# Strassen's algorithm for the second product of a fused attention and feed-forward kernel

## The chip, the cores and the metric

The kernel runs on one core of a Trainium2 chip. TensorE multiplies into PSUM (the memory of its results), VectorE and ScalarE work on the results, and in the traces the matmuls of TensorE, and the instructions of VectorE, ran in the order in which the program issued them: in the kernel before, the matmuls of M piece 0 end at 396.70, ScalarE copies its half, and VectorE comes to the other half at 399.74, behind the chain issued before it. The metric is the device time of one execution in microseconds. A profiled execution gives the trace; its span, from first to last instruction, is about 1.8 us shorter than the time. The profiler also records the clock granted to TensorE, as a share of full speed; in the traces it is 1.00 or 0.50 at any time.

In the views PE is TensorE, PEld its loads of weights, DVE VectorE, ACT ScalarE and POOL GpSimd; L408 is line 408 of that run's kernel. A line of a timeline gives start, length, engine, line, operation, tile written <- tiles read, shapes and count, then in brackets the idle time before it and what ended that.

## The reference, cut to what matters

```python
# x: (8, 8, 512, 64), state: (8, 8, 32, 64)     B, H, S, D and 32 states
xread = softmax(x @ state.T / 8) @ state         # every token reads the states
sread = softmax(state @ x.T / 8) @ x             # every state reads the tokens
t = concat([xread, sread])                       # per batch 512 + 32 tokens of 8 * 64 = 512
h = t @ w_in                                     # (4352, 512) @ (512, 2048)
out = (h * sigmoid(1.702 * h)) @ w_out           # second product: (4352, 2048) @ (2048, 512)
```

Everything is float32.

## The kernel before

The first product of a batch doesn't multiply the tokens by `w_in`. It multiplies the states by `w_in` first (the tiles M, four pieces a batch) and then the softmax weights by M. The second product is a plain sum over 16 pieces G of the hidden layer, one PSUM buffer of 128x512 for each of four row blocks of 128 tokens:

```python
def down(key, r, fs, dst, last):
    ...
    for f in fs:
        nc.tensor.matmul(ops, G[key, f][:, P * r : P * (r + 1)], w_out[:, f],
                         start=(f == 0), stop=(f == NF - 1))       # 128x128 by 128x512
    if fs[-1] == NF - 1:
        nc.scalar.copy(osb, ops)
        nc.gpsimd.dma_start(dst, osb)
```

The attention of the next batch is threaded into this product. It is cut into 16 slots, each behind four pieces of one row block:

```python
at(0, att_state, b)                  # transpose of the states
for j in range(NPR): at(1 + j, att_xT, b, j)
at(5, att_scores, b); at(5, att_blocks, b); at(5, att_s_max, b); at(5, att_s_exp, b)
at(5, att_x_exp, b); at(5, att_s_norm, b); at(5, att_x_norm, b)    # softmax, mostly on VectorE
for c in range(NFC - 1): at(7 + c, att_M, b, c)                    # M pieces 0, 1, 2
for g in range(NG): at(11 + g, att_eT, b, g)
at(14, att_sread, b)
```

Each piece of M fills two PSUM buffers, which the attention work shares (there are only two; the scores alone have others), and is copied out by VectorE and ScalarE in turn:

```python
def copies(b, i):
    return nc.scalar.copy if b in (0, 1) or i % 2 else nc.vector.tensor_copy

def att_M(b, c):
    ...
    ps = [att_ps([P, FC], f"M_{b}_{c}_{g}") for g in range(NG)]    # 2 buffers in all
    by_state(b, ps, lambda rows, j: w_in[c][rows, j])              # 16 matmul instructions of 64x32
    for g in range(NG):
        copies(b, g)(m[:, g], ps[g])                               # g = 0: VectorE, g = 1: ScalarE
```

Of the kernel before, what the change touches and what calls it, by code (L numbers as in the profile page):

```python
# [10 lines left out]
FP32 = mybir.dt.float32  # L11
I32 = mybir.dt.int32
U32 = mybir.dt.uint32
AF = mybir.ActivationFunctionType
ALU = mybir.AluOpType
# [5 lines left out]
def kernel(  # L21
# [23 lines left out]



    nc = tc.nc

    B, H, S, D = x.shape  # L50
    Ns = state.shape[2]
    DM = H * D
    DF = moe_w_in.shape[1]
    P = 128
    NPR = P // Ns
    NG = H // NPR
    NF = DF // P
    SCH = S // P
    ST = S + Ns
    FC = 512  # L60
    NFC = DF // FC
    NB = S // Ns
    scale = float(1.0 / np.sqrt(D))
    eps = 1e-9
    assert (NG * D, NPR * Ns, NPR * P, DM, NFC) == (P, P, DM, FC, SCH)

    out_x = out.rearrange("(b t) n -> b t n", b=B)[:, :S].rearrange("b (c q) n -> b c q n", c=SCH)
    out_s = out.rearrange("(b t) n -> b t n", b=B)[:, S:]
# [1 line left out]
    st_v = state.rearrange("b (j g) n d -> b g j n d", g=NG)  # L70

    konst = ctx.enter_context(tc.tile_pool(name="konst", bufs=1))
    xpool = ctx.enter_context(tc.tile_pool(name="xpool", bufs=2))
    apool = ctx.enter_context(tc.tile_pool(name="apool", bufs=1))
    mpool = ctx.enter_context(tc.tile_pool(name="mpool", bufs=3))
    wpool = ctx.enter_context(tc.tile_pool(name="wpool", bufs=2))
    gpool = ctx.enter_context(tc.tile_pool(name="gpool", bufs=1))
    opool = ctx.enter_context(tc.tile_pool(name="opool", bufs=2))
    psA = ctx.enter_context(tc.tile_pool(name="psA", bufs=2, space=bass.MemoryType.PSUM))
    psH = ctx.enter_context(tc.tile_pool(name="psH", bufs=2, space=bass.MemoryType.PSUM))  # L80
    psO = ctx.enter_context(tc.tile_pool(name="psO", bufs=4, space=bass.MemoryType.PSUM))
# [8 lines left out]



    free = [gpool.tile([P, S], FP32, name=f"g_{i}") for i in range(NF + 9)]
    zeros = free[-1].bitcast(mybir.dt.bfloat16)[:, :FC]
    nc.vector.memset(zeros, 0.0)
    one = konst.tile([P, 1], FP32, name="one")
# [9 lines left out]
    xn, stn = {}, {}  # L106
# [4 lines left out]
            nc.sync.dma_start(stn[b][:, g], st_v[b, g])  # L111

    def load_x(b):
        xn[b] = xpool.tile([P, SCH, H, D], FP32, tag="xn", name=f"xn_{b}")
        for c in range(SCH):
            queue = nc.scalar if b == 0 and c % 2 else nc.sync
            queue.dma_start(xn[b][:, c], x_v[b, c])
# [6 lines left out]
    w_out = konst.tile([P, NF, DM], FP32, name="w_out")  # L124
    w_in_words, w_out_words = moe_w_in.bitcast(I32), moe_w_out.bitcast(I32)

    PIECES = [("i", c, k) for c in range(NFC) for k in range(NPR)] + [("o", f) for f in range(NF)]
    raw, power = {}, {}
    AHEAD = 3

    def load_weight(i):

        key = PIECES[i]
        nin, room = NFC * NPR, NF // 2
        if i < room or nin - NPR <= i < nin:
            o = 2 * (i % room if i < room else i - (nin - NPR))
            raw[i] = w_out[:, o : o + 2].rearrange("p f n -> p (f n)").bitcast(I32)
        else:
            raw[i] = wpool.tile([P, 2 * FC], I32, tag="raw", name="raw_" + "_".join(map(str, key)), bufs=4)
        if key[0] == "i":  # L140
            _, c, k = key
            src = w_in_words[P * k : P * (k + 1), 2 * FC * c : 2 * FC * (c + 1)]
        else:
            src = w_out_words[P * key[1] : P * (key[1] + 1)]
        nc.sync.dma_start(raw[i], src)
# [7 lines left out]
    for i, v in enumerate((8.0 * most, 8.0 * (most - least))):  # L153
        t = konst.tile([P, 1], FP32, name=f"edge_{i}")
# [3 lines left out]
    def words(i):  # L158
        w = raw[i].rearrange("p (n w) -> p w n", w=2)
        return w[:, 0].bitcast(U32), w[:, 1]  # L160

    def round_a(i):

        _, hi = words(i)
        sc = wpool.tile([P, FC], I32, tag="sc", name=f"sc_{i}", bufs=AHEAD + 1)
        power[i] = sc
        nc.vector.tensor_scalar(sc, hi, 0x7FF00000, None, ALU.bitwise_and)
        if PIECES[i][0] == "o":
            nc.vector.tensor_scalar(sc, sc, most, least, ALU.min, ALU.max)
            nc.vector.tensor_scalar(sc, sc, -least, 8.0, ALU.add, ALU.mult)  # L170
            return
        nc.scalar.activation(out=sc.bitcast(FP32), in_=sc, func=AF.Relu, bias=edge[0], scale=-8.0)
        nc.scalar.activation(out=sc, in_=sc.bitcast(FP32), func=AF.Relu, bias=edge[1], scale=-1.0)  # L173

    def round_b(i):
        key = PIECES[i]
        dst = w_in[key[1]][:, key[2]] if key[0] == "i" else w_out[:, key[1]]
        fr = dst.bitcast(I32)
        lo, hi = words(i)
        sc = power.pop(i)  # L180

        nc.vector.tensor_scalar(fr, hi, 0xFFFFF, 0x100000, ALU.bitwise_and, ALU.bitwise_or)
        nc.vector.scalar_tensor_tensor(sc, hi, -0x80000000, sc, ALU.bitwise_and, ALU.bitwise_or)  # L183
        nc.vector.scalar_tensor_tensor(dst, lo, 2.0**-32, fr, ALU.mult, ALU.add)  # L184
        nc.vector.scalar_tensor_tensor(dst, dst, 2.0**-20, sc.bitcast(FP32), ALU.mult, ALU.mult)  # L185
        del raw[i]

    done = {"load": 0, "a": 0, "b": 0, "credit": 0.0}

    def load_weights(upto):  # L190
        while done["load"] < min(upto, len(PIECES)):
            load_weight(done["load"])
            done["load"] += 1

    def powers_to(n):
        while done["a"] < min(n, len(PIECES)):
            load_weights(done["a"] + 1)
            round_a(done["a"])
            done["a"] += 1

    def round_to(n, ahead=AHEAD):

        while done["b"] < min(n, len(PIECES)):
            powers_to(min(done["b"] + 1 + ahead, max(NFC * NPR, done["b"] + 1)))
            round_b(done["b"])
            done["b"] += 1
            if done["b"] > NPR:
                load_weights(done["b"] + 2 * NPR)

    def pace(pieces):  # L210

# [13 lines left out]
    A = {b: {} for b in range(B)}  # L225
# [33 lines left out]
    def att_blocks(b):  # L259

        a = A[b]
        t = apool.tile([P, NG, NB, Ns], FP32, tag="e1", name=f"e1_{b}")
        a["e1"] = t
# [27 lines left out]

    NS1 = NG * NB

# [57 lines left out]

    def att_slots(b):

        slots = [[] for _ in range(4 * SCH)]

        def at(i, fn, *args):
            slots[i].append((fn, args))

        at(0, att_state, b)
        for j in range(NPR):  # L360
            at(1 + j, att_xT, b, j)
        at(5, att_scores, b)
        at(5, att_blocks, b)
        at(5, att_s_max, b)
        at(5, att_s_exp, b)
        at(5, att_x_exp, b)
        at(5, att_s_norm, b)
        at(5, att_x_norm, b)
        for c in range(NFC - 1):
            at(7 + c, att_M, b, c)  # L370
        for g in range(NG):
            at(11 + g, att_eT, b, g)
        at(14, att_sread, b)
        return slots


    G = {}
# [10 lines left out]
    def up_x(b, f, spare=False):  # L388
        c, o = divmod(P * f, FC)
        m = A[b]["M", c]  # L390
        up(b, f, S, [m[:, g, o : o + P] for g in range(NG)], [A[b]["aT"][:, g] for g in range(NG)], spare)

    def up_s(f):
        up(
            "sr", f, B * Ns,
            [w_in_of(k, f) for k in range(NPR)],
            [srT[:, k].rearrange("p b n -> p (b n)") for k in range(NPR)],
        )
# [3 lines left out]
    def down(key, r, fs, dst, last):  # L402

        if fs[0] == 0:
            O[key, r] = psO.tile([P, DM], FP32, tag="o", name=f"o_{key}_{r}")
        ops = O[key, r]
        for f in fs:
            nc.tensor.matmul(  # L408
                ops, G[key, f][:, P * r : P * (r + 1)], w_out[:, f], start=(f == 0), stop=(f == NF - 1)
            )  # L410
            if last:
                free.append(G.pop((key, f)))
        if fs[-1] == NF - 1:
            osb = opool.tile([P, DM], FP32, tag="osb", name=f"osb_{key}_{r}")
            nc.scalar.copy(osb, ops)  # L415
            nc.gpsimd.dma_start(dst, osb)  # L416


    nper = FC // P
# [75 lines left out]
    for f in range(NF):  # L495
# [11 lines left out]
        if f % 2 == 1:  # L507
            up_x(1, rest.pop(0))
    load_state(2)
    load_x(2)  # L510

    nb = P // Ns
    for b in range(1, B):
        ahead = b + 1 < B
        slots = att_slots(b + 1) if ahead else [[]] * (4 * SCH)
        if not ahead:
            for f in range(NF):
                up_s(f)
            for r in range(B // nb):
                for i in range(4):  # L520
                    down("sr", r, range(4 * i, 4 * i + 4), out_s[nb * r : nb * (r + 1)], r == B // nb - 1)
        if b > 1:
            for f in range(NF):
                if f == 2 * nper:
                    att_M(b, NFC - 1)
                up_x(b, f)
        for u in range(4 * SCH):
            r, i = divmod(u, 4)
            down(b, r, range(4 * i, 4 * i + 4), out_x[b, r], r == SCH - 1)
            for fn, args in slots[u]:  # L530
                fn(*args)
        if b + 2 < B:
            load_state(b + 2)
            load_x(b + 2)
# [30 lines left out]
```

## Time and profile before

| | before |
|---|---|
| time, median (lowest to highest) | 862.65 us (862.49 to 864.99) |
| TensorE busy | 98% of the span |
| second product, 7 batches | 54.9 us each |
| second product, states | 27.5 us |
| one batch, from second product to second product | 95.0 us |
| granted TensorE clock, mean | 0.996 |

TensorE's busy time says little of its speed: the ends of matmuls are modelled, and neighbours overlap in the listing (the states' second product, listed from 743.88 for 27.63 us, would end at 771.51, and the next product starts at 771.34). So durations of a stage are read here as differences of starts. The 95.0 us are 269.98 - 174.99, two starts of a batch's second product. The lines themselves are in the prediction.

### The profile page before, as it was taken

The numbers are of one execution on the slowest core, as the hardware profiler recorded it, in microseconds if no ns is written. First come the engines' busy times: TensorE is split into PE (matmuls) and PEld (weight loads), VectorE is DVE, ScalarE is ACT, GpSimd is POOL, SyncE is SP. The second block draws the span as 40 slices with busy tenths as digits, with TensorE's granted clock in tenths as the row PEclk, the third lists the DMA queues.
The fourth block names the chain that finished last, engine by engine and source line by source line (L and its number), as shares of the span: only waits on it lengthen the run. The fifth ranks groups of instructions, "written<-read, shape, count | busy, mean of one in ns | idle before, by whom it ended". The sixth has DMA issues, their size and how long they took to land.

```text
span 860.6 us, 6881 instructions
## 1 busy us (share of the span) xinstructions
PE 841.0 (98%) x2898; PEld 391.0 (45%) x2900; DVE 215.9 (25%) x402; ACT 205.5 (24%) x347; POOL 19.8 (2%) x42
## 2 busy tenths in 40 slices
PE   8987999999999999999999999999999999999997
PEld 3332554443544445443544445443544348644443
DVE  4996996005000320005000510014000500000000
ACT  3686211012032212302041212302131202103100
POOL 0000000010000000000000000000000000000000
PEclk9999999999999999999999999999999999999999
DMA  9620345010030002000020002000000000000000
GB/s 246 248 82 17 123 150 125 1 64 13 12 62 4 12 25 61 1 16 13 25 49 4 24 13 62 0 13 12 17 8 4 22 12 13 1 14 11 12 12 25
DMA packets 43135, 35.05 MB, mean 41 GB/s; under 512 B 36832, under 2 KB 36832, under 8 KB 43104
## 3 DMA queue, kind: packets, MB, share of 16 engines
q1 hardware_dynamic: 37920, 25.17, 10.7%
q0 software_dynamic: 3104, 8.92, 2.9%
q10 hardware_dynamic: 2080, 0.52, 0.3%
q8 instruction: 23, 0.38, 0.2%
q14 instruction: 8, 0.07, 0.0%
HBM read 25.69 MB, written 8.91 MB: 40 GB/s over the span
## 4 chain that ended last, share of the span: by engine, by line
issue 72%; PE 21%; DVE 2%; POOL 2%; ACT 2%; DMA 1%; SPq 0%; POOLq 0%; ACTq 0%
PE o L408 11%; PE h L383 7%; POOL out_dram L416 2%; PE M L252 1%; PE sr L341 1%; DMA xn<-in_x_dram 1%; PE xT L244 0%; ACT M L324 0%; PE s L252 0%; ACT e L282 0%; DVE w_in L185 0%; DVE w_in L184 0%; DVE sc L183 0%; PE warm L103 0%; ACT sc L173 0%
## 5 line engine op out<-in xcount | busy, mean ns | idle before, releaser
L408 PE MATMUL o<-w_out,g 128*128 128x512 f32 x1024 | 456.9, 595 | 0.0
L408 PEld LDWEIGHTS o<-w_out,g 128*128 128x128 f32 x1024 | 188.6, 190 | 231.7 <-issue 230.3
L383 PE MATMUL h<-aT,M 128*128 128x512 f32 x512 | 227.2, 599 | 9.3 <-ACT M L324 9.3
L383 PEld LDWEIGHTS h<-aT,M 128*128 128x128 f32 x512 | 96.6, 191 | 136.8 <-issue 113.2
L385 ACT ACTIVATE g<-h 128x512 f32<-128x512 f32 x128 | 76.3, 597 | 157.0 <-PE h L383 156.9
L324 DVE COPY M<-M 128x512 f32<-128x512 f32 x24 | 16.4, 682 | 194.6 <-PE M L252 194.6
L415 ACT COPY osb<-o 128x512 f32<-128x512 f32 x32 | 18.8, 586 | 136.3 <-PE o L408 134.0
L324 ACT COPY M<-M 128x512 f32<-128x512 f32 x40 | 22.6, 587 | 66.7 <-PE M L252 66.7
L252 PE MATMUL M<-w_in,stT 64*32 64x512 f32 x512 | 37.8, 601 | 0.4 <-DVE w_in L185 0.4
L416 POOL DMA_DIRECT2D out_dram<-osb x32 | 17.6, 549 | 782.4 <-ACT osb L415 782.2
L245 ACT COPY xT<-xT 128x512 f32<-128x512 f32 x18 | 10.5, 586 | 92.3 <-PE xT L244 92.3
L235 DVE COPY stT<-stT 128x128 f32<-128x128 f32 x6 | 1.8, 292 | 119.5 <-PE stT L233 119.5
L341 PEld LDWEIGHTS sr<-eT,xn 128*128 128x128 f32 x256 | 29.8, 192 | 3.8 <-issue 3.8
L341 PE MATMUL sr<-eT,xn 128*128 128x64 f32 x256 | 29.4, 273 | 0.0
L245 DVE COPY xT<-xT 128x512 f32<-128x512 f32 x14 | 9.7, 692 | 74.5 <-PE xT L244 74.5
L383 PE MATMUL h_sr<-srT,w_in 128*128 128x256 f32 x128 | 27.8, 379 | 0.0
L408 PE MATMUL o_sr<-w_out,g 128*128 128x512 f32 x64 | 27.6, 592 | 0.0
L383 PEld LDWEIGHTS h_sr<-srT,w_in 128*128 128x128 f32 x128 | 24.3, 190 | 3.7 <-issue 0.5
L244 PEld LDWEIGHTS xT<-ident,xn 128*128 128x128 f32 x128 | 16.0, 143 | 17.2 <-issue 13.5
L265 DVE STREAM_TRANSPOSE e<-s 128x512 f32<-128x512 f32 x16 | 10.5, 695 | 47.4 <-PE s L252 47.4
L103 PE MATMUL warm<-g 128*128 128x512 bf16 x74 | 20.9, 431 | 1.5 <-DVE one L97 1.2
L350 DVE COPY srT<-sr 64x128 f32<-64x128 f32 x6 | 1.7, 283 | 81.4 <-PE sr L341 81.4
(63 smaller groups left out, 355.2 us busy)
## 6 DMA issues: line engine op xcount, KB each, us to landing
raw_o<-in_moe_w_out_dram SPq DMA_DIRECT2D x16, 512.0 KB
out_dram<-osb POOLq DMA_DIRECT2D x32, 256.0 KB, 2.3
xn<-in_x_dram SPq DMA_DIRECT2D x30, 256.0 KB
w_out<-in_moe_w_in_dram SPq DMA_DIRECT2D x12, 512.0 KB
raw_i<-in_moe_w_in_dram SPq DMA_DIRECT2D x4, 512.0 KB
stn<-in_state_dram SPq DMA_DIRECT2D x16, 32.0 KB
xn<-in_x_dram ACTq DMA_DIRECT2D x2, 256.0 KB
out_dram<-osb_sr POOLq DMA_DIRECT2D x2, 256.0 KB, 7.1
```

The costliest lines, as they stand in the source:

```text
L103: nc.tensor.matmul(ps, zeros[:, :P], zeros, start=True, stop=True)
L244: nc.tensor.transpose(ps[:, c], x_heads(b, c, j), ident)
L245: copies(b or None, j)(A[b]["xT"][:, j], ps.rearrange("p c q -> p (c q)"))
L252: nc.tensor.matmul(ps[g][st], A[b]["stT"][rows, st], rhs(rows, j), start=True, stop=True)
L265: nc.vector.transpose(t[:, g].rearrange("p i n -> p (i n)"), a["s"][g])
L324: copies(b, g)(m[:, g], ps[g])
L341: nc.tensor.matmul(ps[:, j], x_heads(b, c, j), a["eT"][:, :, c, Ns * j : Ns * (j + 1)], start=(c == 0), stop=(c == SCH - 1),)
L383: nc.tensor.matmul(hps, lhs[i], rhs[i], start=(i == 0), stop=(i == n - 1))
L385: nc.scalar.activation(out=gt[:, :ntok], in_=hps, func=AF.Gelu_apprx_sigmoid)
L408: nc.tensor.matmul(ops, G[key, f][:, P * r : P * (r + 1)], w_out[:, f], start=(f == 0), stop=(f == NF - 1))
L415: nc.scalar.copy(osb, ops)
L416: nc.gpsimd.dma_start(dst, osb)
```

## The change

Strassen's algorithm (in its form with 15 sums) splits tokens, hidden layer and output columns in half and does seven products of halves where the plain form does eight. The sums of quarters of G are made by VectorE for each batch, those of `w_out` once, in float32. Batch 0 keeps the plain form, because its pieces of `w_out` are still being converted while it runs. The core of the diff:

```diff
+    def sums_of_g(key, f, ntok):
+        half = ntok // 2
+        (a11, a21), (_, a22) = quarters(key, f, ntok), quarters(key, HF + f, ntok)
+        s1, s2 = S1[:, f, :half], S2[:, f, :half]
+        nc.vector.tensor_tensor(out=s1, in0=a21, in1=a22, op=ALU.add)
+        nc.vector.tensor_tensor(out=a21, in0=a11, in1=a21, op=ALU.subtract)
+        nc.vector.tensor_tensor(out=s2, in0=s1, in1=a11, op=ALU.subtract)
+
+    def strassen(key, ntok, dst, slots=None):
...
+        def product(ps, lhs, rhs, first):
+            for r in range(nb):                       # 2 row blocks
+                for f in range(HF):                   # 8 pieces, 128x128 by 128x256
+                    nc.tensor.matmul(ps[:, r], lhs[f][:, P * r : P * (r + 1)], rhs[:, f],
+                        start=(first and r == 0 and f == 0), stop=(f == HF - 1), skip_group_check=True)
+                if todo:
+                    for fn, args in todo.pop(0):
+                        fn(*args)                     # attention slots of the next batch
...
+        X = bank("x"); product(X, A(0, 0), B11, True);  nc.scalar.copy(k1, X)
+        Y = bank("y"); product(Y, S(S2), T2, True);     k2 = Y + k1
+        product(X, A(0, 1), B21, False);                store(0, 0, X, None)
+        for f in range(HF): a12[f] -= S2[f]
+        product(Y, A(1, 0), T3, False);                 k3 = Y + k1
+        Z = bank("z"); product(Z, S(S1), T1, True);     store(1, 1, Z, k3)
+        product(Y, A(1, 1), T4, False);                 store(1, 0, Y, k1)
+        product(Z, A(0, 1), B22, False);                store(0, 1, Z, k2)
...
-        slots = [[] for _ in range(4 * SCH)]
+        slots = [[] for _ in range(14)]
...
-            at(1 + j, att_xT, b, j)
+            at(j, att_xT, b, j)
...
-        for c in range(NFC - 1):
-            at(7 + c, att_M, b, c)
+        at(5, att_M, b, 0)
+        at(7, att_M, b, 1)
+        at(9, att_M, b, 2)
         for g in range(NG):
-            at(11 + g, att_eT, b, g)
-        at(14, att_sread, b)
+            at(10 + g, att_eT, b, g)
+        at(12, att_sread, b)
...
+    for t, x0, x1 in ((T1, B12, B11), (T2, B22, T1), (T4, B21, T2), (B12, B22, B12)):
+        nc.vector.tensor_tensor(out=t, in0=x0, in1=x1, op=ALU.subtract)
+    for f in range(HF):
+        sums_of_g(1, f, S)                            # between batch 0 and 1
```

(The lines with k2, k3 and a12 are written short here; each is a VectorE instruction, the last one eight.) The rest finds room in SBUF: one buffer of x instead of two, the raw weights in a tile that later holds the sums, and loads of weights issued by the state of their buffer.

More of the change, by code (lines that the diff above doesn't have):

```diff
@@ L62 @@
     NB = S // Ns
+    HF, HN = NF // 2, DM // 2
     scale = float(1.0 / np.sqrt(D))
@@ L72 @@
     konst = ctx.enter_context(tc.tile_pool(name="konst", bufs=1))
-    xpool = ctx.enter_context(tc.tile_pool(name="xpool", bufs=2))
+    xpool = ctx.enter_context(tc.tile_pool(name="xpool", bufs=1))
     apool = ctx.enter_context(tc.tile_pool(name="apool", bufs=1))
     mpool = ctx.enter_context(tc.tile_pool(name="mpool", bufs=3))
-    wpool = ctx.enter_context(tc.tile_pool(name="wpool", bufs=2))
     gpool = ctx.enter_context(tc.tile_pool(name="gpool", bufs=1))
@@ L89 @@
     make_identity(nc, ident)
-    free = [gpool.tile([P, S], FP32, name=f"g_{i}") for i in range(NF + 9)]
+    free = [gpool.tile([P, S], FP32, name=f"g_{i}") for i in range(NF)]
+    sums = konst.tile([P, 3, HF * HN], FP32, name="sums")
+    T1, T2, T4 = (sums[:, i].rearrange("p (f n) -> p f n", f=HF) for i in range(3))
+    free += [sums[:, 1 + i // 4, S * (i % 4) : S * (i % 4 + 1)] for i in range(8)]
+    later = konst.tile([P, 12, S], FP32, name="later")
     zeros = free[-1].bitcast(mybir.dt.bfloat16)[:, :FC]
@@ L113, in load_x @@
     def load_x(b):
-        xn[b] = xpool.tile([P, SCH, H, D], FP32, tag="xn", name=f"xn_{b}")
+        if b == 1:
+            xn[b] = sums[:, 0].rearrange("p (c h d) -> p c h d", c=SCH, h=H)
+        else:
+            xn[b] = xpool.tile([P, SCH, H, D], FP32, tag="xn", name=f"xn_{b}")
         for c in range(SCH):
@@ L138, in load_weight @@
         else:
-            raw[i] = wpool.tile([P, 2 * FC], I32, tag="raw", name="raw_" + "_".join(map(str, key)), bufs=4)
+            o = 2 * (i % 4)
+            raw[i] = later[:, o : o + 2].rearrange("p f n -> p (f n)").bitcast(I32)
         if key[0] == "i":
@@ L164, in round_a @@
         _, hi = words(i)
-        sc = wpool.tile([P, FC], I32, tag="sc", name=f"sc_{i}", bufs=AHEAD + 1)
+        sc = later[:, 8 + i % (AHEAD + 1)].bitcast(I32)
         power[i] = sc
@@ L188, with before @@
     done = {"load": 0, "a": 0, "b": 0, "credit": 0.0}
+    def before(i):
+        nin = NFC * NPR
+        return i - (nin - NPR if i < nin else 2 * NPR if i < nin + NPR else NPR)
     def load_weights(upto):
@@ L206, in round_to @@
             done["b"] += 1
-            if done["b"] > NPR:
-                load_weights(done["b"] + 2 * NPR)
+            while done["b"] > NPR and done["load"] < len(PIECES) and before(done["load"]) < done["b"]:
+                load_weights(done["load"] + 1)
     def pace(pieces):
@@ L410, in down @@
             )
-            if last:
+            if last and f < HF:
                 free.append(G.pop((key, f)))
@@ L416, in down, with quarters @@
             nc.gpsimd.dma_start(dst, osb)
+    S1, S2 = (later[:, 4 * i : 4 * i + 4].rearrange("p f n -> p (f n)").rearrange("p (f t) -> p f t", f=HF) for i in range(2))
+    p1, u2, u3 = (later[:, 8 + i] for i in range(3))
+    def quarters(key, f, ntok):
+        g, half = G[key, f], ntok // 2
+        return g[:, :half], g[:, half:ntok]
+    def sums_of_g(key, f, ntok):
[5 more added lines that the diff above has]
+        nc.vector.tensor_tensor(out=s2, in0=s1, in1=a11, op=ALU.subtract)
@@ new lines, in strassen, with bank, kept, store @@
+    def strassen(key, ntok, dst, slots=None):
+        half = ntok // 2
+        nb = half // P
+        B11, B21, B22 = w_out[:, :HF, :HN], w_out[:, HF:, :HN], w_out[:, HF:, HN:]
+        T3 = w_out[:, :HF, HN:]
+        A = lambda i, k: [quarters(key, HF * k + f, ntok)[i] for f in range(HF)]
+        S = lambda t: [t[:, f, :half] for f in range(HF)]
+        todo = list(slots or [])
+        def bank(name):
+            return psO.tile([P, nb, HN], FP32, tag="o", name=f"{name}_{key}")
+        def product(ps, lhs, rhs, first):
+            for r in range(nb):
+                for f in range(HF):
+                    nc.tensor.matmul(
+                        ps[:, r], lhs[f][:, P * r : P * (r + 1)], rhs[:, f],
+                        start=(first and r == 0 and f == 0), stop=(f == HF - 1), skip_group_check=True,
+                    )
+                if todo:
+                    for fn, args in todo.pop(0):
+                        fn(*args)
+        def kept(t):
+            return t[:, : nb * HN].rearrange("p (r n) -> p r n", r=nb)
+        def store(i, k, ps, with_):
+            o = opool.tile([P, nb, HN], FP32, tag="osb", name=f"osb_{key}_{i}{k}")
+            for r in range(nb):
+                if with_ is None:
+                    nc.scalar.copy(o[:, r], ps[:, r])
+                else:
+                    nc.vector.tensor_tensor(out=o[:, r], in0=ps[:, r], in1=with_[:, r], op=ALU.add)
+                nc.gpsimd.dma_start(dst(nb * i + r, slice(HN * k, HN * (k + 1))), o[:, r])
+        k1, k2, k3 = kept(p1), kept(u2), kept(u3)
+        X = bank("x")
+        product(X, A(0, 0), B11, True)
+        nc.scalar.copy(k1, X)
+        Y = bank("y")
+        product(Y, S(S2), T2, True)
+        nc.vector.tensor_tensor(out=k2, in0=Y, in1=k1, op=ALU.add)
+        product(X, A(0, 1), B21, False)
+        store(0, 0, X, None)
+        for f in range(HF):
+            a12 = quarters(key, HF + f, ntok)[0]
+            nc.vector.tensor_tensor(out=a12, in0=a12, in1=S2[:, f, :half], op=ALU.subtract)
+        product(Y, A(1, 0), T3, False)
+        nc.vector.tensor_tensor(out=k3, in0=Y, in1=k1, op=ALU.add)
+        for f in range(HF):
+            free.append(G[key, f])
+        Z = bank("z")
+        product(Z, S(S1), T1, True)
+        store(1, 1, Z, k3)
+        product(Y, A(1, 1), T4, False)
+        store(1, 0, Y, k1)
+        product(Z, A(0, 1), B22, False)
+        store(0, 1, Z, k2)
+        for f in range(HF, NF):
+            free.append(G[key, f])
@@ L510 @@
     load_x(2)
+    B11, B12, B21, B22 = (w_out[:, HF * i : HF * (i + 1), HN * k : HN * (k + 1)] for i in range(2) for k in range(2))
+    for t, x0, x1 in ((T1, B12, B11), (T2, B22, T1), (T4, B21, T2), (B12, B22, B12)):
+        nc.vector.tensor_tensor(out=t, in0=x0, in1=x1, op=ALU.subtract)
+    for f in range(HF):
+        sums_of_g(1, f, S)
     nb = P // Ns
@@ L514 @@
         ahead = b + 1 < B
-        slots = att_slots(b + 1) if ahead else [[]] * (4 * SCH)
         if not ahead:
@@ L518 @@
                 up_s(f)
-            for r in range(B // nb):
-                for i in range(4):
-                    down("sr", r, range(4 * i, 4 * i + 4), out_s[nb * r : nb * (r + 1)], r == B // nb - 1)
+                if f >= HF:
+                    sums_of_g("sr", f - HF, B * Ns)
+            strassen("sr", B * Ns, lambda r, n: out_s[nb * r : nb * (r + 1), :, n])
         if b > 1:
             for f in range(NF):
-                if f == 2 * nper:
+                if f == nper + 1:
                     att_M(b, NFC - 1)
                 up_x(b, f)
-        for u in range(4 * SCH):
-            r, i = divmod(u, 4)
-            down(b, r, range(4 * i, 4 * i + 4), out_x[b, r], r == SCH - 1)
-            for fn, args in slots[u]:
-                fn(*args)
+                if f >= HF:
+                    sums_of_g(b, f - HF, S)
+        strassen(b, S, lambda r, n: out_x[b, r][:, n], att_slots(b + 1) if ahead else None)
         if b + 2 < B:
```

## The prediction

> **What bounds the kernel now.** I read the page first, for which engine fills the span.
>
> ```profile
> PE 841.0 (98%) x2898; PEld 391.0 (45%) x2900; DVE 215.9 (25%) x402; ACT 205.5 (24%) x347; POOL 19.8 (2%) x42
> ...
> L408 PE MATMUL o<-w_out,g 128*128 128x512 f32 x1024 | 456.9, 595 | 0.0
> ...
> L383 PE MATMUL h<-aT,M 128*128 128x512 f32 x512 | 227.2, 599 | 9.3 <-ACT M L324 9.3
> ```
>
> TensorE is busy 98% of the span and VectorE a quarter. The second product (L408) is more than half of it: 1024 instructions are 512 products of 128x128 by 128x512, so every float32 product is two matmul instructions. Then I took the timeline of TensorE in the last batch, which holds nothing but this work:
>
> ```profile
> 716.25 27.79 PE L383 MATMUL h_sr<-srT,w_in 128*128 128x256 f32 x128
> 743.88 27.63 PE L408 MATMUL o_sr<-w_out,g 128*128 128x512 f32 x64
> ...
> 800.02 55.10 PE L408 MATMUL o<-w_out,g 128*128 128x512 f32 x128
> ```
>
> Starts are what counts, because the listed ends overlap. 128 instructions of 512 columns take 54.95 us (the modelled last end trimmed), 0.429 us each. The first line is the key one: 128 instructions of 256 columns, each with its own weight load, take 743.88 - 716.25 = 27.63 us, 0.2159 us each. The change uses just this shape. It needs a weight load every 0.216 us; in that stage the loads were busy 24.3 of 27.6 us and left no gap, so they stay hidden, with little to spare.
>
> The third reading is the inner rhythm of a batch[...]. Timeline of TensorE, then of VectorE, while batch 3's attention is worked out:
>
> ```profile
> 387.53 1.09 PE L252 MATMUL s<-xT,stT 64*32 64x512 f32 x16
> 388.55 7.13 PE L408 MATMUL o<-w_out,g 128*128 128x512 f32 x16
> 395.61 1.09 PE L252 MATMUL M<-w_in,stT 64*32 64x512 f32 x16
> 396.63 3.70 PE L408 MATMUL o<-w_out,g 128*128 128x512 f32 x8
> 400.26 1.27 PE L252 MATMUL M<-w_in,stT 64*32 64x512 f32 x16
> ```
> ```profile
> 388.74 1.31 DVE L265 STREAM_TRANSPOSE e<-s 128x512 f32<-128x512 f32 x2 [7.72 <-PE s L252]
> ...
> 397.32 1.23 DVE L311 TENSOR_TENSOR e<-e,sm 128x1024 f32<-128x1024 f32 x1
> 398.57 1.25 DVE L313 STREAM_TRANSPOSE aT<-e 128x1024 f32<-128x1024 f32 x1
> 399.74 0.65 DVE L324 COPY M<-M 128x512 f32<-128x512 f32 x1
> ```
>
> VectorE's softmax chain runs from the end of the scores to 399.8, and only then does its queue reach the copy of M piece 0, done at 400.4. M piece 1 reuses that PSUM buffer (two of them), and its 16 matmuls took 1.27 us instead of 1.09: it came just when the buffer was let go, 0.18 us early. This chain is already the second limit, hidden by exact spacing.
>
> [...] In the trace independent neighbours start some 0.08 us before the listed end of the one before (0.34 us steps for listed 0.42)[...]. [...]
>
> ```profile
> 80.20 1.09 PE L252 MATMUL M<-w_in,stT 64*32 64x512 f32 x16
> 85.52 8.83 PE L383 MATMUL h<-aT,M 128*128 128x512 f32 x16 [4.23 <-ACT M L324]
> ```
> ```profile
> 87.00:89.00 2.00, 2.00 (x4) 0.75 (x3) 1.97 (x5) 0.26 (x1) 0.00 (x0) 0.50 0.00 0
> ```
>
> (The second fence is the windows view; the third figure from the right is the granted clock, 0.50.) After 4.23 us of idle the next 16 matmuls took 8.83 us where 7.13 is usual: 1.7 us more. A gap of 2.12 us earlier was followed by the usual 7.13. [...]
>
> **The change part by part.**
>
> *Products.* Seven products of 2 row blocks by 8 pieces are 112 products of 256 columns, 224 instructions: 224 x 0.2159 = 48.36 us, against 128 x 0.429 = 54.93. Saved 6.57 us a batch, 46.0 us for seven. The states: 112 instructions x 0.2159 = 24.18 against 27.46 (the distance 743.88 to 771.34), saved 3.3. Gross 49.3 us, all on TensorE's path. (An eighth less multiplication saves 12%; it can't save more.)
>
> *Sums of G.* [...] Hidden, except by its order in the queue, next.
>
> *The attention slots.* Slots are now a row block of 8 pieces, 16 x 0.216 = 3.45 us, as long as before. But M piece 0 moves from slot 7 to slot 5, right behind the scores, and piece 1 from slot 8 to 7. On the old clock: scores start 387.53, M0 388.55, second half of the Y bank from 389.57 for 32 x 0.216 = 6.91 plus 0.2 (the first matmul after an M waits for its weights, as 3.63 instead of 3.43 us between M starts shows). M1 is then reached at 396.7. Its buffer still comes free at 400.4, because M0's copy stands behind the same softmax chain, to which nothing is taken away. TensorE stalls 3.7 to 3.8 us. In the old order 11.7 us lay between M0's earliest possible place and M1; in the new one 8.1. This happens in batches 1 to 6: 6 x 3.75 = +22.5 us; the old 0.18 goes, 6 x 0.18 = -1.1.
>
> *Between batch 0 and 1.* Four adds of 2048. T1 runs at 142.7, where VectorE falls idle after the last rounding; T2 after the piece f = 11 of batch 0 (156). T4 overwrites G pieces 12 to 15, read until 173.3[...] then the copy of the state transpose of batch 2[...]. TensorE starts X at 174.99, does slot 0, and reaches slot 1 (a transpose that needs that copy's buffer) at 182.5. [...]
>
> *Small.* Extra starts of short groups, +1; end of the kernel, two adds and two transfers in place of a copy and one, +0.3; clock halved after some of the seven stalls. [...] Loads, buffers of x (one instead of two) and the head: the reload waits for the state read at slot 12 and has the 28 us of the next first product, against 3 to 4 us of issue; 0.
>
> Sum: 862.7 - 46.0 - 3.3 - 1.1 + 22.5 + 3.9 + 1.0 + 0.3 + 1.3 = 841.3 us.
>
> **Rivals.** (a) *No stall at M1*, the whole gross gain comes: about 818. For it: the change moved M0 early on purpose, as if to spread the copies. Against: VectorE's order and the 0.18 us in the old trace. (b) *Stalls beget slow clock.* [...] each of seven stalls costs 1.7 more: 852. For it: 4.23 us sufficed once, and 3.75 lies close. Against: 2.12 did not[...]. (c) *Weight loads become the bound*: at 88% of TensorE's time a slip of 5% in 224 instructions a batch is 17 us, 858. Against: the 128 instructions of the states' first product ran without a gap. (d) *Late sums*: the A12 adds come after the chain, so the third product into Y may wait for its sum. [...]
>
> **Range and chances.** Most weight is on the stall near 3.75 and little clock loss, 838 to 844. Rival (a) in part (a shorter chain) pulls to 829, (b) or (c) in part to 853. 2% faster means below 845.4, which the central case makes by 4 us; that gives 0.67. Slower by 2% would need 70 us of new waits: 0.01.
>
> **What would show it.** TensorE's spacing in the products 0.216 us with weight loads about 88% busy; the products of seven batches and of the states near 7 x 48.4 + 24.2 = 363 us in all. A gap of 3.7 us before M in six batches, released by VectorE's copy of M; about 4 us before the transpose of x of batch 2. Clock 1.00 nearly throughout. No wait of TensorE on the sums from batch 2 on. The prediction is wrong if the copy of M comes earlier than the chain's end, if the spacing isn't 0.216, or if a gap stands at another product.

The forecast's sum came to 841.3 us. The wait between batch 0 and 1, +3.9, and the slow clock, +1.3, stand in the sum as bare figures; without them it comes to 836.1. The +1.0 and +0.3 of the small terms are estimates, without a working. The sums are, for a batch, 24 adds of 256 elements, 8 more for A12 - S2, two of 512 and six stores of 256; in the changed kernel's trace an add of 256 takes 0.42 us, one of 512 0.69 and one of 2048 2.29.

## The result and the profile after

The changed kernel takes 855.35 us (median; the runs lie between 854.75 and 855.69). Ratios in this document are the mean time of one kernel's fast runs over that of the other's of the same rounds, so not quite the ratio of the medians. Here it is 0.9908, with a 95% interval of 0.989 to 0.9926: 0.9% faster. The predicted 841.3 was 14 us too low and the range ended at 853.

The page first:

```profile
PE 809.6 (95%) x3620; PEld 536.8 (63%) x3620; DVE 344.5 (40%) x723; ACT 195.5 (23%) x340; POOL 35.9 (4%) x72
...
PEclk9999899989999999999899999998999999999998
...
L271 PE MATMUL M<-w_in,stT 64*32 64x512 f32 x512 | 47.0, 659 | 17.8 <-DVE M L343 17.4
```

TensorE's share fell from 98 to 95%. The clock row, 40 slices of 21 us, has five 8s, where the kernel before had 9s throughout; a short dip in a slice still reads as 9 (3.4 us at half clock leave a mean of 0.92), so an 8 stands for a long one (6.8 us leave 0.84). (The first of the five lies in the first 107 us and the last behind the last matmul; the three between belong to waits that the change brought.) And the M matmuls, which before had 0.4 us of idle in front of them, now have 17.8, ended by VectorE's copy of M.

The arithmetic came as worked out. The last batch, timeline of TensorE:

```profile
797.44 7.07 PE L471 MATMUL x<-w_out,g 128*128 128x256 f32 x32
804.35 7.07 PE L471 MATMUL y<-sums,later 128*128 128x256 f32 x32
...
838.88 7.07 PE L471 MATMUL z<-w_out,g 128*128 128x256 f32 x32
```

Each product takes 6.91 us, 0.2159 us an instruction, and all seven 838.88 + 6.91 - 797.44 = 48.35 us. The states' seven take 24.18.

The inside of a batch is where it went. Timeline of TensorE while batch 3's attention is worked out (it is the place that the prediction shows for the kernel before), then of VectorE at the same place one batch earlier:

```profile
300.07 1.06 PE L271 MATMUL M<-w_in,stT 64*32 64x512 f32 x16
301.06 7.17 PE L471 MATMUL y<-w_out,g 128*128 128x256 f32 x32
308.17 1.04 PE L271 MATMUL M<-w_in,stT 64*32 64x512 f32 x2
312.11 1.85 PE L271 MATMUL M<-w_in,stT 64*32 64x512 f32 x14 [2.90 <-DVE M L343]
313.89 8.05 PE L471 MATMUL z<-sums,later 128*128 128x256 f32 x32
321.88 1.09 PE L271 MATMUL M<-w_in,stT 64*32 64x512 f32 x16
```
```profile
216.75 1.25 DVE L332 STREAM_TRANSPOSE aT<-e 128x1024 f32<-128x1024 f32 x1
217.92 0.65 DVE L343 COPY M<-M 128x512 f32<-128x512 f32 x1
218.50 2.75 DVE L503 TENSOR_TENSOR g<-g,later 128x256 f32<-128x256 f32 x8
```

M piece 0 follows the scores at once. Piece 1 is reached at 308.17, gets two of its 16 matmul instructions out, and waits until 312.11 for the buffer that VectorE empties only after the softmax chain. The listed idle of 2.90 us is counted from the modelled end; from start to start it is 3.94. What the prediction had not in this size is the second half: behind the gap, the last 14 small matmuls take 1.85 us instead of about 1, and the product into Z 8.05 instead of 7.17. From 312.11 to 321.88 are 9.77 us, where the same work at full clock takes 8.12 (a later run, gap_shortest: 303.44 to 311.56). The view of windows says why; the third figure from the right is the granted clock:

```profile
220.50:223.50 3.00, 3.00 (x8) 2.34 (x8) 1.95 (x5) 0.00 (x0) 0.00 (x0) 0.50 0.00 0
312.70:315.90 3.20, 3.20 (x19) 1.67 (x6) 3.20 (x9) 0.59 (x1) 0.00 (x0) 0.53 0.02 5
405.00:411.00 6.00, 5.45 (x22) 3.08 (x23) 4.37 (x11) 0.59 (x1) 0.00 (x0) 0.50 0.00 0
```

Three batches, three dips to half the clock, and so in all six; each lasts 3.4 or 6.8 us. The wait between batch 0 and 1 does the same:

```profile
179.80 3.62 PE L471 MATMUL x<-w_out,g 128*128 128x256 f32 x16
188.13 1.12 PE L263 MATMUL xT<-ident,xn 128*128 128x128 f32 x4 [4.71 <-DVE stT L254]
189.04 5.50 PE L471 MATMUL y<-sums,later 128*128 128x256 f32 x16
```

The transpose could have come at 183.25. It came at 188.13, and the 16 matmuls behind it took 5.50 us instead of 3.62.

An account of the spans, 860.6 before and 853.9 after, so -6.7:

| what | worked out from | us |
|---|---|---|
| seven batches of products | 7 x (48.35 - 54.93) | -46.1 |
| states | 24.18 - 27.46 | -3.3 |
| waits before M piece 1 | 6 gaps of 3.95, start to start, less 6 x 0.18 of before | +22.6 |
| wait between batch 0 and 1 | 188.13 - 183.25 | +4.9 |
| slow stretch behind the six waits | 60.55 from restart to M piece 2, less 6 x 8.12 | +11.8 |
| slow stretch behind the wait in batch 1 | 6.24 from the transpose to the next, where a later run has 3.89 | +2.3 |
| until the first Strassen product | 175.80 against 174.99 | +0.8 |
| after the last product | 8.1 against 5.7 | +2.4 |
| cheaper slots | below, 6 x 0.4 | -2.3 |
| sum | | -6.9 |

### The profile page after: what moved, and what is told of

Same layout as the page of the kernel before. It is cut to its first block, busy times and chain, and to the rows that moved or that the text cites. A ratio compares the mean times of both kernels' runs of the same rounds, so it can differ in the third digit from the quotient of the medians.

```text
span 853.9 us, 8775 instructions
## 1 busy us (share of the span) xinstructions
PE 809.6 (95%) x3620; PEld 536.8 (63%) x3620; DVE 344.5 (40%) x723; ACT 195.5 (23%) x340; POOL 35.9 (4%) x72
## 4 chain that ended last, share of the span: by engine, by line
issue 69%; PE 19%; DVE 5%; POOL 4%; ACT 2%; DMA 1%; SPq 0%; POOLq 0%; DVEq 0%
PE h L403 7%; PE o L428 6%; POOL out_dram L490 4%; PE z L471 1%; PE y L471 1%; PE M L271 1%; PE sr L360 1%; PE x L471 1%; DMA xn<-in_x_dram 1%; PE xT L263 0%; DVE g L453 0%; ACT M L343 0%; PE s L271 0%; ACT e L301 0%; DVE w_in L199 0%
## 5 line engine op out<-in xcount | busy, mean ns | idle before, releaser
L471 PE MATMUL x<-w_out,g 128*128 128x256 f32 x448 | 100.0, 379 | 0.0
L471 PEld LDWEIGHTS x<-w_out,g 128*128 128x128 f32 x448 | 84.2, 190 | 13.9 <-issue 3.4
L271 PE MATMUL M<-w_in,stT 64*32 64x512 f32 x512 | 47.0, 659 | 17.8 <-DVE M L343 17.4
L471 PEld LDWEIGHTS z<-sums,later 128*128 128x128 f32 x224 | 47.5, 215 | 16.7 <-issue 9.1
L471 PE MATMUL z<-sums,later 128*128 128x256 f32 x224 | 57.7, 422 | 0.0
L471 PE MATMUL y<-sums,later 128*128 128x256 f32 x224 | 52.4, 389 | 0.0
L471 PE MATMUL y<-sums,g 128*128 128x256 f32 x224 | 51.1, 382 | 0.0
L471 PE MATMUL z<-w_out,g 128*128 128x256 f32 x224 | 50.8, 381 | 0.0
L471 PE MATMUL y<-w_out,g 128*128 128x256 f32 x224 | 50.1, 382 | 0.0
L471 PEld LDWEIGHTS y<-w_out,g 128*128 128x128 f32 x224 | 42.1, 190 | 10.5 <-issue 5.0
L471 PEld LDWEIGHTS y<-sums,later 128*128 128x128 f32 x224 | 43.1, 197 | 5.7
```

The source lines that it names most:

```text
L271: nc.tensor.matmul(ps[g][st], A[b]["stT"][rows, st], rhs(rows, j), start=True, stop=True)
L471: nc.tensor.matmul(ps[:, r], lhs[f][:, P * r : P * (r + 1)], rhs[:, f], start=(first and r == 0 and f == 0), stop=(f == HF - 1), skip_grou ...
```

## The experiments

Theory A: VectorE's copy of M piece 0, queued behind the softmax chain, makes TensorE wait in six batches; VectorE's sums between batch 0 and 1 make it wait once; and each wait costs a second time through the halved clock. Rivals: R1, the slow matmuls behind the gap come from VectorE's adds on A12, which run just then (218.50 to 221.2 above) and use the same memory; R2, a wait that is taken away only moves on; R3, the wait comes from the added VectorE work and not from the slots.

| run | time, us | before, us | ratio (95%) |
|---|---|---|---|
| m0_copy_act | 821.12 | 862.49 | 0.9507 (0.9485 to 0.9529) |
| gap_filled | 841.85 | 862.49 | 0.9754 (0.9732 to 0.9776) |
| batch1_early | 847.74 | 862.49 | 0.9818 (0.9798 to 0.9837) |
| before_m_early | 896.76 | 862.49 | 1.0386 (1.0367 to 1.0404) |
| both_mended | 813.47 | 864.76 | 0.9411 (0.9391 to 0.9431) |
| gap_shorter | 844.14 | 864.76 | 0.976 (0.9741 to 0.9779) |
| m_slots_late | 823.88 | 864.76 | 0.9529 (0.9511 to 0.9547) |
| gap_shortest | 827.46 | 862.64 | 0.9593 (0.9572 to 0.9613) |
| mended_head_filled | 810.77 | 862.64 | 0.9392 (0.9375 to 0.9408) |

All nine gave correct outputs.

### m0_copy_act: who copies M piece 0

```diff
-            copies(b, g)(m[:, g], ps[g])
+            (nc.scalar.copy if c == 0 else copies(b, g))(m[:, g], ps[g])
```

> One edit to the changed kernel: both halves of M piece 0 are copied out of PSUM by ScalarE, whose queue is free of the softmax chain, in batches 2 to 7 (the halves that VectorE had). Theory A (M piece 1 waits for VectorE's copy behind the softmax chain, and each wait then costs a slow clock): the six gaps of 3.9 us and the six slow stretches after them go, 6 x 3.85 + 12.4 = 35.5 us less, about 820 us. Rival R1 (the slow matmuls after the gap come from VectorE's adds on A12 reading the same memory, not from the clock): the gaps go but the slow stretch stays, about 855.4 - 23 = 832. Rival R2 (the wait only moves on, to the sum that the third product into Y needs or to bank Z): less than 10 us gained, above 845.

It took 821.12 us, where theory A had 820, R1 832 and R2 over 845. The timeline of TensorE in batch 1:

```profile
208.72 7.17 PE L471 MATMUL y<-w_out,g 128*128 128x256 f32 x32
215.82 1.09 PE L271 MATMUL M<-w_in,stT 64*32 64x512 f32 x16
216.84 7.17 PE L471 MATMUL z<-sums,later 128*128 128x256 f32 x32
```

No gap before M piece 1, and the product into Z takes its 7.17 us. Only an engine was exchanged for one copy a batch; it is worth 34 us. Nothing else waits in its place, so R2 is out for this copy.

### gap_filled: the wait kept, TensorE kept at work

```diff
+    fill = konst.tile([P, FC], mybir.dt.bfloat16, name="fill")      # zeros
+    def fill_gap(n):
+        ps = psH.tile([P, FC], FP32, tag="h", name="fill")
+        for _ in range(n):
+            nc.tensor.matmul(ps, fill[:, :P], fill, start=True, stop=True)
...
+        at(7, fill_gap, 17)
         at(7, att_M, b, 1)
...
+            if b == 2 and j == 1:
+                at(1, fill_gap, 21)
             at(j, att_xT, b, j)
```

> The changed kernel with dummy bf16 matmuls of zeros put on TensorE just where it waits: 17 ahead of M piece 1 in each of six batches (3.7 us), 21 ahead of the transpose in batch 1 (4.5 us). Nothing that TensorE waits for comes sooner. Theory A (clock): the waits stay, the slow stretches of together 12.4 + 2.35 = 14.7 us go, so about 841, and the granted clock has no dip after batch 0. Rival R1 (the adds of VectorE slow the matmuls): the adds still fall on the same products, so no change, 855. If the fill itself overshoots the gaps, each 1 us of it shows as 6 us of time.

It took 841.85 us: 13.5 us less than the changed kernel, though it does more work and nothing that it waits for comes sooner. Timeline of TensorE in batch 1, then of VectorE, then the view of windows for the product into Z there:

```profile
211.60 3.62 PE L121 MATMUL fill<-fill 128*128 128x512 bf16 x16
215.15 1.36 PE L278 MATMUL M<-w_in,stT 64*32 64x512 f32 x16
216.44 7.17 PE L481 MATMUL z<-sums,later 128*128 128x256 f32 x32
```
```profile
215.30 2.75 DVE L513 TENSOR_TENSOR g<-g,later 128x256 f32<-128x256 f32 x8
```
```profile
216.50:223.50 7.00, 7.00 (x35) 5.94 (x32) 2.75 (x7) 0.59 (x1) 0.00 (x0) 1.00 0.01 2
```

VectorE's eight adds on A12 run from 215.30 to 218.05, over the start of the product into Z, and its matmuls keep their 7.17 us at a clock of 1.00 (third figure from the right). So R1 is out: the adds are there and the matmuls are not slow. It is also nearly the prediction's own figure: with the clock kept, the kernel is within 1 us of 841.3, though in part by luck, because the prediction's other misses cancel (see below). A kernel that computes zeros to wait faster is a measurement and not a mend, of course.

### batch1_early: VectorE's order between batch 0 and 1

```diff
-    for t, x0, x1 in ((T1, B12, B11), (T2, B22, T1), (T4, B21, T2), (B12, B22, B12)):
+    for t, x0, x1 in ((T1, B12, B11), (B12, B22, B12), (T2, B22, T1)):
         nc.vector.tensor_tensor(out=t, in0=x0, in1=x1, op=ALU.subtract)
-    for f in range(HF):
+    for f in range(HF - 1):
         sums_of_g(1, f, S)
+    nc.vector.tensor_tensor(out=T4, in0=B21, in1=T2, op=ALU.subtract)
+    sums_of_g(1, HF - 1, S)
```

> The changed kernel with VectorE's work between batch 0 and 1 in another order: T1, T3, T2 and seven of eight groups of sums of G ahead of T4, which alone has to wait for the end of batch 0. Theory A: the wait of 4.9 us before the transpose of batch 2's x goes, and with it the slow stretch of 2.35 us: 7.2 us less, about 848. Rival R1 (no clock effect): 4.9 less, 850.5. Rival: the sums then run in the last pieces of batch 0 and delay its own work: 855 or more.

It took 847.74 us, 7.6 less than the changed kernel; theory A had 7.2, the rival without the clock 4.9. In its timeline the transpose of batch 2's x starts at 184.00, right behind its 16 matmuls from 180.54, and the next 16 take 3.62 us. Only T4 and the last group of sums, which comes behind it, need the end of batch 0; the other work had stood behind T4 for no reason but order. Against the kernel before, this run is 1.8% faster, and the interval of the ratio (0.9798 to 0.9837) leaves open whether it reaches 2%.

### before_m_early: the slots alone, without Strassen

```diff
 # in the kernel before
-        for c in range(NFC - 1):
-            at(7 + c, att_M, b, c)
+        at(5, att_M, b, 0)
+        at(7, att_M, b, 1)
+        at(9, att_M, b, 2)
```

> The kernel before, with nothing but the slots of M moved as the change moves them: piece 0 right behind the scores, piece 1 two slots later, piece 2 two more. No Strassen, no sums on VectorE. Theory A: the same wait before M piece 1 comes up in six batches, 3.7 us each, and the slow clock behind it, about 2 us each: 862.7 + 6 x 5.7 = 897. Rival R1 (slow stretch only with the adds present): the wait alone, 862.7 + 22 = 885. Rival R3 (the wait comes from the extra VectorE work of the change, not from the slots): no change, 863.

It took 896.76 us, where theory A had 897, R1 885 and R3 863. Three moved lines cost the old kernel 34 us, as much as m0_copy_act gives back to the new one. A batch in its timeline of TensorE:

```profile
305.35 1.04 PE L252 MATMUL M<-w_in,stT 64*32 64x512 f32 x2
309.33 1.95 PE L252 MATMUL M<-w_in,stT 64*32 64x512 f32 x14 [2.94 <-DVE M L324]
311.22 9.00 PE L409 MATMUL o<-w_out,g 128*128 128x512 f32 x16
```

The gap is the same 3.98 us, and behind it 16 matmuls of 512 columns take 9.00 us instead of 7.13. There are no sums on VectorE here at all, so R3 is out, and R1 once more. In this run five of the six gaps had a dip of the clock behind them, the one in batch 1 had none.

### m_slots_late: TensorE asks later

```diff
-        at(5, att_M, b, 0)
-        at(7, att_M, b, 1)
-        at(9, att_M, b, 2)
+        at(7, att_M, b, 0)
+        at(9, att_M, b, 1)
+        at(10, att_M, b, 2)
         for g in range(NG):
-            at(10 + g, att_eT, b, g)
-        at(12, att_sread, b)
+            at(11 + g, att_eT, b, g)
+        at(13, att_sread, b)
```

> The changed kernel with M pieces 0, 1, 2 back at slots 7, 9, 10, the transposes of e at 11 and 12 and the state read at 13: VectorE's order of work stays, only TensorE asks later. Theory A: piece 1 is asked for 15 us after the scores, its buffer comes free at 14.7 (the adds on A12 now stand before the copy), so the gaps and the slow clock go as with ScalarE's copy: 820 to 822. Rival R2 (the wait moves on): the copies queue behind the adds and piece 2 or the transposes of e wait, 830 or more.

It took 823.88 us, on a chip where the kernel before took 864.76; the ratio 0.9529 overlaps that of ScalarE's copy, 0.9507, and times 862.65 it is 822.0, where theory A had 820 to 822. So there are two ways to the same end: bring the copy forward, or ask for the buffer later. The one wait that this run has in addition is 0.7 us in front of the states' first product, which now follows the state read at once.

### both_mended: both waits gone

The edits of m0_copy_act and batch1_early together.

> The changed kernel with both mends at once: M piece 0 copied by ScalarE, and VectorE's work between batch 0 and 1 reordered. Theory A: the two gains add, 821.1 - 7.5 = 813.6, between 812 and 816; that is the 49.3 us of the products and hardly anything lost, so it beats both kernels. Rival: the seven products hold a cost of their own (sums, weight loads) that the waits had hidden, then 820 or more.

It took 813.47 us, ratio 0.9411 to the kernel before, and beats both kernels. The gains add up. A batch, from second product to second product, takes 265.67 - 177.82 = 87.85 us in its trace, 7.14 less than the 94.99 of before. The products give 6.57 of that and the old wait 0.18; the other 0.4 lies in the slots, where the scores and M piece 0 now follow each other directly. In batch 1 of that trace the product into Y starts at 202.37, M piece 1 at 209.48 and the product into Z at 210.50, without a gap.

### gap_shorter and gap_shortest: how long a wait the clock bears

In gap_shorter VectorE's copy of M piece 0 comes ahead of the last transpose of the chain, in gap_shortest ahead of its last multiplication too. `att_x_turn` is the part that was cut off:

```diff
         at(5, att_M, b, 0)
+        at(5, att_x_turn, b)
```

The expectations tell three suppositions apart, none of which a trace had shown: rule 1, half clock comes only behind a whole step of the clock (3.413 us, as measured below) without a matmul; rule 2, it comes behind a step with few of them too, and the small M matmuls count little; rule 3, it comes behind every gap over 2.5 us. (Where they were put into words in the record, rules 1 and 2 are cut.)

> The changed kernel with VectorE's copy of M piece 0 put ahead of the last transpose of the softmax chain (1.25 us), so the six gaps shrink from 3.9 to about 2.65 us and nothing else moves. Rule 1 [...]: no dip in those batches, 855.4 - 6 x 1.25 - 12.4 = 835.5. Rule 2 [...]: some of the six still dip, half of them gives 842. Rule 3 (any gap over 2.5 us): all six dip, 848.

> As the run with the shorter gap, with the copy of M piece 0 put ahead of the chain's last multiplication too: the six gaps shrink to about 1.45 us. In the run with 2.7 us five of six gaps had a dip of the clock behind them. If a little activity keeps the clock, none of the six dips: 855.4 - 6 x 2.45 - 12.4 = 828. If the light M matmuls count as idle and any such stretch can dip, all six: 840. Half of them: 834.

Timeline of TensorE at the same place in both, gap_shorter first:

```profile
305.46 1.04 PE L271 MATMUL M<-w_in,stT 64*32 64x512 f32 x2
308.14 1.09 PE L271 MATMUL M<-w_in,stT 64*32 64x512 f32 x14 [1.64 <-DVE M L347]
309.16 8.85 PE L476 MATMUL z<-sums,later 128*128 128x256 f32 x32
```
```profile
302.07 1.04 PE L271 MATMUL M<-w_in,stT 64*32 64x512 f32 x2
303.44 1.09 PE L271 MATMUL M<-w_in,stT 64*32 64x512 f32 x14 [0.33 <-DVE M L350]
304.46 7.17 PE L479 MATMUL z<-sums,later 128*128 128x256 f32 x32
```

With gaps of 2.7 us five of six had a dip, and the time was 844.14, between the expectations for three dips and for six (on the slower chip of the two). With gaps of 1.4 us none had, and the time was 827.46, as expected for none. The five dips of gap_shorter are less than five independent cases: they start 92.16 us apart each time, 27 of the steps of 3.413 us that the next paragraph shows, so that each gap stood at the same place in a step. Nor do they refute rule 1 by themselves, if small matmuls are not to count: from 305.46 to 309.16, 3.70 us, TensorE had nothing but those of M.

The traces hold more on the clock than these two runs. In each trace, every dip that ends before the last matmul starts and stops on one grid of steps of 3.413 us (to within 0.01 us), so the clock changed step by step. Two steps of that grid, from gap_shorter and from m_slots_late, by the view of windows (the figures behind the comma are the time TensorE was busy and its matmuls):

```profile
42.92:46.33 3.41, 1.38 (x3) 0.68 (x4) 3.34 (x8) 2.43 (x5) 0.00 (x0) 1.00 0.01 2
183.35:186.76 3.41, 1.41 (x7) 0.90 (x5) 3.31 (x10) 0.00 (x0) 0.00 (x0) 1.00 0.00 0
```

The step behind the first had a clock of 0.50, that behind the second 1.00. In the ten traces without a fill in the head, between 14 and 700 us, 849 steps at full clock held large matmuls (128x128 weights, 256 or 512 columns) alone or none: the 12 that a dip followed had up to 1.39 us of matmuls (the first line above, with its edges rounded), the other 837 had 1.41 us or more. So a step ahead of a dip needn't be idle, which puts rule 1 out; large matmuls for 1.41 us of 3.41, about two fifths, and more kept the clock.

### mended_head_filled: the same mend in the first 90 us

Both mends, and dummy matmuls in two waits that all these kernels have while the first weights come in:

```diff
     att_M(1, 0)
+    fill_gap(10)
...
     att_M(0, 3)
+    fill_gap(19)
```

> The kernel with both mends, and dummy matmuls in two waits that every kernel here has before batch 1's first product is through: 10 in the gap of 2.1 us, 19 in that of 4.2 us. Both were followed by a halved clock in the run with both mends (16 matmuls in 8.83 us instead of 7.13, twice). Clock theory: 2 x 1.7 = 3.4 us less, a ratio to before near 0.937 where both mends alone had 0.941, about 810. If the fill is without use there, 813.

In the trace both stretches of 16 matmuls take 7.13 us, where both_mended had 8.83 twice, and the clock has no dip before the end. The time is 810.77 us, ratio 0.9392. The intervals of the two ratios (0.9375 to 0.9408, and 0.9391 to 0.9431) overlap, so the times do not show that the 3.4 us are gained; it is the fastest kernel by its median only.

## Why the prediction was wrong

- **Products: right.** 48.36 and 24.18 us were worked out from the old kernel's stage with 256 columns; 48.35 and 24.18 came. Weight loads stayed hidden at 190 ns in every 216, so rival (c) fell.
- **Wait before M piece 1: right, place, cause and size.** 6 x 3.75 was predicted, 6 x 3.95 came. before_m_early and m0_copy_act show the cause: the slots, and VectorE's order. Rival (a) fell.
- **Wait between batch 0 and 1: right in kind, 3.9 predicted, 4.9 came.** The sums of G took 187.79 - 178.75 = 9.0 us, where 24 equal steps of 0.34 us, which was the author's estimate, make 8.2: the second add of each group overwrites what the first reads, and starts 0.45 to 0.46 us behind it, while all others start 0.33 to 0.35 us behind the one before. That is most of the 1.0 us; the old trace already had steps of 0.46 us between dependent instructions (L167 and L169 at 121.41 and 121.87, the second reading what the first wrote).
- **Clock: this is the step that failed.** The prediction gave +1.3 us for all seven waits together, less than the 1.7 us that one dip had cost in the old trace. It had the consequence, as rival (b), but mis-sized the chance, which was the author's estimate and not shown by any trace. All seven waits were followed by a dip, and they cost 11.8 + 2.3 = 14.1 us, 12.8 more than predicted, of an error of 14.0. gap_filled shows it by taking away the dips alone: 841.85 us. So rival (b), with its 852, was close to what came. Two readings were at fault. Matmuls close to a gap were taken to keep the clock, while in the changed kernel's own trace the step ahead of batch 1's dip, 216.73 to 220.14, had 1.50 us of matmuls, 0.5 of them of the product into Z. If a step needs 1.40 us of 3.41, a gap of 3.75 us between large matmuls leaves one too idle at about nine in ten places of the grid: (3.41 - 2.01) + (3.75 - 2.01) = 3.14 of 3.41 us (an estimate from the steps above, with the small M matmuls left out). And each was counted at 1.7 us where some dips lasted two steps: the half clock lasted 3.4 us after four of the gaps of 3.9 us and 6.8 us after the other two and after the gap of 4.9 us, and the six cost 2.0 us each on average.
- The old trace had offered one gap of 4.23 us with a dip and one of 2.12 us without. The second was read as a limit. In the changed kernel's trace the very same gap of 2.12 us in the head was followed by 16 matmuls in 8.83 us. It was chance, in that the grid lay otherwise: the changed kernel's step ahead of that dip had 1.29 us of matmuls, while the old kernel's two steps around the gap had 2.88 and 1.82.
- **Small terms.** Extra starts of short groups were given +1.0 and came as -2.3; the end of the kernel was given +0.3 and came as +2.4. From the last product's end to the last instruction the new kernel takes 8.1 us, of which the adds and the issue of two transfers are 2; why the rest is longer than before wasn't tried. Until the first Strassen product it lost 0.8 us where 0 was given. With the waits, the misses outside the clock are +1.2, +1.0, +0.8, +2.1 and -3.3 us, +1.8 in all: that they nearly cancel is luck.
- **Late sums (rival d): right, no wait.** In the changed kernel's trace none of TensorE's waits is for a sum.

What stays open is how the small M matmuls (64x32) and the transposes count for the clock. A step with 1.77 us of M alone was followed by a dip (gap_shorter, 305.75), one with 0.69 us of large matmuls and 1.02 of M was not (before_m_early, 209.20). No run was made to separate this.

## What to carry to other kernels

A cut in arithmetic shortens the time that other engines' chains had to hide in, and every reuse of a buffer must be checked against the new clock: ask in each queue what stands in front of the copy that frees it. A wait of TensorE of more than some 2 us can be paid twice, once as a gap and once as half clock behind it. Over all traces here that came after none of 6 gaps of 1.4 us, 5 of 6 of 2.7 and 17 of 18 of 3.9 (start to start), and after 6 of 10 of 2.1 us and all 15 of 4.2 us or more (idle as listed); so when you estimate a wait near 4 us, count the second payment in full. Where a gain of 49 us arrives as 7, look for the few instructions in the wrong queue before giving up the algorithm: one copy given to another engine and VectorE's sums between batch 0 and 1 put in another order brought it back.
